# Two more token tiles turned by DMA instead of TensorE, one weight load moved back, and two gate tiles moved forward

## The chip, the cores and the metric

The kernel runs on one core of one Trainium2 chip. The metric is the device time of one execution in microseconds (us); of several runs the median is given. A profile is one profiled execution of the same program; it has a time of its own.

## The reference

`x` has 2048 tokens of 512 values; `xn` is its layer norm. The output is `x + A(xn) + B(xn)`.

- A is a sliding local attention: `q`, `k`, `v` are `xn @ wqkv`, 32 heads of 16 values; each token attends to itself and to 7 tokens before it at a distance of 2 each (mask, softmax, sum); then `@ wo`.
- B is a gated unit with a spatial matrix: `z = gelu(xn @ w_in)` has two halves of 688 values. The first half is `z1`; the second is layer-normed over its 688 values to `z2`. Then `g = w_sp @ z2 + b_sp` mixes the tokens (2048 x 2048), and B is `(z1 * g) @ w_out`.

```python
xn = _layernorm(x, axis=-1)
return x + _A_ref(xn, A_wqkv, A_wo) + _B_ref(xn, B_w_in, B_w_sp, B_b_sp, B_w_out)
```

## The kernel before

**Tiles and stages.** The tokens are 16 tiles of 128. Everything stays on the chip between the stages.

1. *Norm and turn.* `x` is loaded in nine DMAs (`x0` to `x12`, lines 162 to 166). For tile i, VectorE takes mean and variance (`b`, `ag`), GpSimd the reciprocal root (`gr`), and VectorE writes the normalised tile into one of eight buffers (`n`, line 180; tiles 8 to 15 take the buffers of tiles 0 to 7 again, line 194). Matmuls need the tile turned, channels on the partitions, in `xnT`. Tiles below `NPE` (8) are turned by TensorE: four 128x128 turns into a PSUM bank (`T`, line 213), and ScalarE copies them out (`Tc`, line 216). The other tiles are turned by one DMA each (`t`, line 196) from SP's queue.
2. *z and y.* For each tile eight matmuls with 344 columns (line 231) make z2's half (`z`), and eight more make z1's half (`y`); ScalarE applies gelu (`h`, line 249, and `yg`, line 313). They need the weights `wz0`, `wz1` (ScalarE's queue) and `wy` (SP's queue).
3. *q, k, v.* Eight passes each (`k0` to `k7` and so on, line 324), 64 matmuls to a pair of dimensions; each pass needs all sixteen tiles of `xnT` and its weights (`wk`, `wq`, `wv`, lines 241 to 243). The copies out of PSUM are `kc`, `qc`, `vc` (line 337). Since the attention reaches over tile borders, small DMAs copy the halos (`kh0` to `kh3`, `vh`, lines 342 and 343).
4. *Attention on VectorE.* Products of q and k (`m`, line 358), folds (`f`, partly adding DMAs from GpSimd, line 366), logits (`p`), maximum (`X`), softmax, and the weighted sum of v (`a`, lines 425 to 438).
5. *Spatial mixing.* `M0` to `M15`, 32 matmuls each (line 467), with `w_sp` loaded and turned by eight DMAs (`W0` to `W7`, line 451) into three buffers; ScalarE adds the bias (`G`), VectorE multiplies with z1 (`g`), and a DMA turns the product (`U`, lines 473 to 476).
6. *Output.* `gf`, `re` and `ao` (lines 511, 516 and 523) add both parts in PSUM, then x is added and the result stored.

**What sets the order.** It is written out by hand. Five lists (`pe`, `act`, `dve`, `pool`, `sp`, lines 565 to 612) name the steps of each engine in order; each step has a list of steps that it needs, and the program is issued so that each engine gets its list. A step waits only for what it needs, but whatever follows it in the same list waits too. DMAs of one queue are issued in the order of the list, and SP's list holds the x loads, most weight loads, the transposes `t` and `W`, the halos of the first two k chunks and of v, the turns `U` and the stores.

PSUM holds three buffers of two banks (`mm`) for z, y, q, k, v and M, and two buffers of one bank (`aux`) for the turns. A buffer goes round: the fourth user waits for the reader of the first (`psum`, line 201). So the order of z and y tiles in TensorE's list also says whose gelu each one waits for.

Around the change TensorE's list is `T5 z4 T6 z5 T7 B z6 z7 y0 y1 z8 ... z14 k0`; `B` is the turn of the spatial bias (line 459), which ScalarE copies (`Bc`, line 461). SP's list is `... wk wq wv t8 ... t15 W0 kh0 W1 kh1 vh W2 ...`. `gf0` and `gf1` name the last users of the PSUM buffers that they take over (`EVM`, line 527).

Of the kernel before, what the change touches and what calls it, by code (L numbers as in the profile page):

```python
# [16 lines left out]
NT = S // P  # L17
# [25 lines left out]
def kernel(  # L43
# [15 lines left out]
    G = nc.gpsimd  # L59
# [3 lines left out]
    x2 = A_x.rearrange("b s d -> (b s) d")  # L63
# [42 lines left out]
    z2 = z2_r[:].rearrange("p (i f) -> p i f", i=NT)  # L106
# [43 lines left out]
    def op_(name, after, f):  # L150
        assert name not in do, name
        do[name], needs[name] = f, list(after)

    def tok(i):
        return f"Tc{i}" if i < NPE else f"t{i}"

    NPE = 8
    ALLX = [tok(i) for i in range(NT)]
    ALLN = [f"n{i}" for i in range(NT)]

# [18 lines left out]
    def norm(eng, i):  # L179
        eng.tensor_scalar(xn[i % 8], xs[:, i, :], mv[:, i, 0:1], rstd[:, i:i + 1], ALU.subtract, ALU.mult)  # L180
# [5 lines left out]
    for i in range(NT):  # L186
# [6 lines left out]
        else:  # L193
            op_(f"n{i}", [f"gr{i}"] + ([tok(i - 8)] if i >= 8 else []), lambda i=i: norm(V, i))
        if i >= NPE:
            op_(f"t{i}", [f"n{i}"], lambda i=i: SP.dma_start_transpose(xnT[:, :, i * P:(i + 1) * P], xn[i % 8]))
# [311 lines left out]
    def gated_full(i, start, stop, c=slice(0, D)):  # L508
        th, t0 = i // 8, (i % 8) * P
        for m in range(MF):  # L510
            PE.matmul(po[i][:, c], uT[th][:, m, t0:t0 + P], wout[:, m, c], start=(start and m == 0), stop=(stop and m == MF - 1))  # L511

    def gated_rest(tiles, start, stop):
        for i in tiles:
            r, t0 = 64 * (i // 2 % 2), (i % 8) * P
            PE.matmul(po[i], uT[i // 8][r:r + FREST, MF, t0:t0 + P], wout[r:r + FREST, MF, :],  # L516
                      start=start, stop=stop, tile_position=(r, 0))
# [6 lines left out]
                          start=(start and d == 0), stop=(stop and d == DH - 1), tile_position=(32 * g, 0))  # L524

    U = [[f"U{j}" for j in range(8 * th, 8 * th + 8)] for th in range(2)]
    EVM = [f"G{j}" for j in range(NT)] + ["Bc", "Tc4"]
    for n in (0, 1):
        op_(f"gf{n}", LO + U[0] + EVM, lambda n=n: [gated_full(i, True, False) for i in groups[n]])
        op_(f"re{n}", [f"gf{n}"], lambda n=n: gated_rest(groups[n], False, False))  # L530
# [28 lines left out]
    for n, c in enumerate(halves):  # L559
# [2 lines left out]
        op_(f"Sl{n}", [f"Fl{n}"], lambda n=n, c=c: (SP, A)[n].dma_start(out2[i * P:(i + 1) * P, c], o_of(i)[:, c]))  # L562


    pe = """wu T0a T0 z0a z0A T1 z0B T2 z1 T3 z2 T4 z3 T5 z4 T6 z5 T7 B z6 z7 y0 y1 z8 z9 z10 z11 z12 z13 z14
        k0 k1 q0 q1 z15 k2 k3 q2 q3 k4 k5 q4 q5 k6 k7 q6 q7
        v0 v1 v2 v3 v4 v5 v6 v7 y2 y3 y4 y5 y6 y7 y8 y9 y10 y11 y12 y13 y14 y15
        M0 M1 M2 M3 M4 M5 M6 M7 M8 M9 M10 M11 M12 M13 M14 M15
# [1 line left out]
    for n in pe:  # L570
# [19 lines left out]
    op_("GL", [], lambda: A.preload_act_table(ACT.Gelu_apprx_tanh))  # L590
    op_("EL", ["yg15"], lambda: A.preload_act_table_set("natural_log_exp_and_others"))

    act = """wz0 wz1 GL Tc0a Tc0 Tc1 Tc2 h0 Tc3 h1 Tc4 h2 Tc5 h3 Tc6 h4 Tc7 Bc h5 h6 h7 yg0 yg1 h8 h9 sq8 h10 h11 sq9 h12 h13 h14 sq10
        kc0 sq11 kc1 qc0 sq12 qc1 h15 kc2 sq13 kc3 sq14 qc2 sq15 qc3 kc4 kc5 qc4 qc5 kc6 kc7 qc6 qc7
        vc0 zn8 vc1 zn9 vc2 zn10 vc3 zn11 vc4 zn12 vc5 zn13 vc6 zn14 vc7 zn15
        yg2 yg3 yg4 yg5 yg6 yg7 yg8 yg9 yg10 yg11 yg12 yg13 yg14 yg15 EL
# [3 lines left out]
    for i in range(6, NT):  # L600
# [5 lines left out]
    OUT = [i for n in range(3) for i in groups[n]] + tail[:3]  # L606
    dve += [f"F{i}" for i in OUT] + ["Fl0", "Fl1"]
    pool = ["b16"] + [f"gr{i}" for i in range(NT)] + "zr0 zr4 f01 zr8 kh2 f10 zr12 kh3 f11 f20 f21 f30 f31".split()
    sp = """x0 x1 x2 x3 x4 x5 x6 x8 wy x12 wk wq wv t8 t9 t10 t11 t12 t13 t14 t15 W0 kh0 W1 kh1 vh
        W2 W3 LO0 LO1 W4 U0 W5 LO2 LO3 U1 U2 W6 LO4 U3 U4 W7 U5 U6 U7 U8 U9 U10 R0 U11 U12 U13 R1 U14 U15""".split()  # L610
    sp += [f"S{i}" for i in OUT] + ["Sl0"]
    act.append("Sl1")
# [52 lines left out]
```

## Time and profile before

| | |
|---|---|
| three runs | 201.16, 201.68 and 201.68 us, median 201.68 |
| the profiled execution | 201.17 us |
| its span, first to last instruction | 199.4 us |
| TensorE busy | 97% of the span |
| VectorE busy | 89% |
| ScalarE busy | 45% |
| mean traffic of the DMA engines | 163 GB/s |

The difference between the profiled execution's time and its span lies outside the program's instructions. In the profile PE is TensorE's matmuls and PEld its weight loads, DVE is VectorE, ACT ScalarE, POOL GpSimd and SP SyncE; a small q behind an engine is its instruction queue, which issues the DMAs. A row of the timeline and of the chain gives the start and the length in us; `x8` behind it says how many instructions it holds. "DMA to landing" is the time from the issue of a DMA to its semaphore. A row of a stretch gives its length, then for each engine the busy time and the number of instructions, then the clock granted to TensorE, the DMA share and GB/s.

### The profile page before, as it was taken

How to read it: one execution, taken by the hardware profiler on the slowest of the kernel's cores; microseconds unless marked ns; L12 is line 12 of the kernel's file. 1: busy time of each engine (PE TensorE's matmuls, PEld its weight loads, DVE VectorE, ACT ScalarE, POOL GpSimd, SP SyncE). 2: the span in 40 equal slices, each digit the busy share in tenths (PEclk: the TensorE clock that was granted, in tenths of full speed). 3: DMA queues.
4: the chain of work that ended last, by engine and by line, in shares of the span. 5: the costliest groups of instructions: out<-in, count | busy, mean ns of one | idle time of the engine just before them, and what ended most of it. 6: DMA issues, size and time to landing. Idle time of an engine off the chain costs nothing.

```text
span 199.4 us, 4530 instructions
## 1 busy us (share of the span) xinstructions
PE 194.3 (97%) x1935; PEld 122.5 (61%) x1935; DVE 177.5 (89%) x204; ACT 89.7 (45%) x130; POOL 39.0 (20%) x67
## 2 busy tenths in 40 slices
PE   7899999999999999999999999999999999999993
PEld 2576666666777766666666666666666654443441
DVE  4999895899898999988999999999999999997234
ACT  2597797795559996672542311112221110043000
POOL 5677122002999330330000000000000000000000
PEclk9999999999999999999999999999999999999999
DMA  5999476840977999998099999999996679914233
GB/s 163 349 361 230 89 123 139 144 81 0 196 132 140 197 196 147 185 167 168 11 234 229 188 168 227 237 123 258 198 230 60 118 219 233 154 19 133 81 105 105
DMA packets 68964, 32.58 MB, mean 163 GB/s; under 512 B 56912, under 2 KB 67024, under 8 KB 68816
## 3 DMA queue, kind: packets, MB, share of 16 engines
q1 hardware_dynamic: 65568, 24.12, 59.5%
q0 software_dynamic: 2176, 7.40, 20.0%
q10 hardware_dynamic: 1200, 0.77, 1.4%
q8 instruction: 15, 0.25, 0.5%
q14 instruction: 5, 0.04, 0.1%
HBM read 10.03 MB, written 2.10 MB: 61 GB/s over the span
## 4 chain that ended last, share of the span: by engine, by line
PE 95%; DMA 3%; DVE 1%; ACTq 0%; DVEq 0%; issue 0%
PE mm L467 37%; PE mm L324 21%; PE mm L231 19%; PE mm L523 7%; PE mm L511 7%; DMA wts<-in_B_w_in_dram 3%; PE aux L511 2%; PE mm L516 1%; PE aux L213 1%; ACTq L239 0%; DVE z L561 0%; DVEq L660 0%; DVE wsp L129 0%; PE aux L523 0%; DVE qk L139 0%
## 5 line engine op out<-in xcount | busy, mean ns | idle before, releaser
L467 PE MATMUL mm<-z,wsp 128*128 128x344 bf16 x512 | 74.8, 309 | 0.0
L467 PEld LDWEIGHTS <-wsp 128*128 128x128 bf16 x512 | 50.1, 98 | 24.6
L324 PE MATMUL mm<-xnT,wts 128*32 128x512 bf16 x768 | 41.9, 380 | 0.0
L231 PE MATMUL mm<-wts,xnT 128*128 128x344 bf16 x256 | 39.0, 309 | 0.5 <-ACT xnT L216 0.5
L324 PEld LDWEIGHTS <-wts 128*32 128x32 bf16 x768 | 29.5, 140 | 12.0 <-issue 0.6
L425 DVE TENSOR_TENSOR prod<-vp,a_sb 128x4096 bf16<-128x4096 bf16 x16 | 36.1, 2285 | 0.0
L481 ACT ACTIVATE qk<-mm,b_col 128x688 bf16<-128x688 f32 x16 | 13.3, 830 | 45.3 <-PE mm L467 38.3
L231 PEld LDWEIGHTS <-xnT 128*128 128x128 bf16 x256 | 24.4, 98 | 13.0 <-issue 1.0
L358 DVE TENSOR_TENSOR prod<-qk 128x4096 bf16<-128x4096 bf16 x12 | 27.0, 2288 | 1.8 <-DMA qk<-qk 1.6
L429 DVE TENSOR_TENSOR prod<-prod,prod 128x8192 bf16<-128x8192 bf16 x6 | 26.5, 4420 | 0.0
L337 ACT CAST qk<-mm 128x1024 bf16<-128x1024 f32 x16 | 16.2, 1012 | 7.8 <-PE mm L324 7.8
L313 ACT ACTIVATE z<-mm 128x688 bf16<-128x688 f32 x16 | 11.8, 748 | 5.7 <-PE mm L231 5.3
L366 POOL DMA_DIRECT2D prod<-prod x10 | 8.7, 1022 | 28.3 <-DVE zvar L282 16.0
L523 PE MATMUL mm<-wts,xnT 32*128 32x512 bf16 x192 | 14.2, 374 | 0.0
L511 PEld LDWEIGHTS <-qk 128*128 128x128 bf16 x85 | 8.2, 98 | 9.4 <-issue 0.8
L511 PE MATMUL mm<-wts,qk 128*128 128x512 bf16 x60 | 13.6, 379 | 0.0
L249 ACT ACTIVATE z<-mm 128x688 bf16<-128x688 f32 x16 | 11.9, 745 | 1.9 <-PE mm L231 1.8
L170 DVE BATCH_NORM_STATS2 stats<-z 128x6 f32<-128x512 bf16 x16 | 10.8, 673 | 1.7 <-DMA z<-in_A_x_dram 1.7
L523 PEld LDWEIGHTS <-xnT 32*128 32x128 bf16 x256 | 6.3, 93 | 7.7 <-issue 0.8
L556 DVE TENSOR_TENSOR z<-mm,wsp 128x512 bf16<-128x512 f32 x6 | 3.8, 684 | 8.0 <-PE mm L523 4.8
L550 ACT CAST z<-mm 128x512 bf16<-128x512 f32 x6 | 3.2, 598 | 13.7 <-PE mm L523 12.3
L177 POOL TENSOR_TENSOR rstd<-rstd,mhalf 128x1 f32<-128x1 f32 x16 | 9.0, 561 | 1.3
(82 smaller groups left out, 169.6 us busy)
## 6 DMA issues: line engine op xcount, KB each, us to landing
prod<-prod POOLq DMA_DIRECT2D x10, 512.0 KB, 7.6
wts<-in_A_wo_dram SPq DMA_DIRECT2D x4, 512.0 KB, 6.3
wsp<-in_A_x_dram SPq DMA_DIRECT2D x2, 1024.0 KB, 6.5
out_dram<-z SPq DMA_DIRECT2D x15, 128.0 KB, 1.8
wts<-in_A_wqkv_dram SPq DMA_DIRECT2D x3, 512.0 KB, 8.6
z<-in_A_x_dram SPq DMA_DIRECT2D x2, 512.0 KB, 6.4
wsp<-z POOLq DMA_DIRECT2D x2, 512.0 KB, 6.5
wsp<-wts POOLq DMA_DIRECT2D x2, 512.0 KB, 8.9
```

The costliest lines, as they stand in the source:

```text
L231: PE.matmul(t[:, hh, 0:FHALF], xnT[:, kc, i * P:(i + 1) * P], w_z[part][:, kc, hh * FHALF:(hh + 1) * FHALF], start=(kc == 0), stop=(kc == ...
L249: A.activation(z2[:, i, :].rearrange("p (a b) -> p a b", a=2), t[:, :, 0:FHALF], ACT.Gelu_apprx_tanh, **total)
L313: op_(f"yg{i}", [f"y{i}"], lambda: A.activation(z1u[:, i, 0:FH].rearrange("p (a b) -> p a b", a=2), t[:, :, 0:FHALF], ACT.Gelu_apprx_tanh))
L324: PE.matmul(t[32 * g:32 * g + 32, dd, :], w, r, start=(kc == 0), stop=(kc == C - 1), tile_position=(0, 32 * g))
L337: op_(f"{a}c{p}", [f"{a}{p}"], lambda: A.copy(home(a, p), t[:].rearrange("p d (t s) -> p d t s", t=2)))
L358: V.tensor_tensor(pr, q, k, ALU.mult)
L425: return lambda: V.tensor_tensor(dst, vp[:, :, th, off:off + GS], a_sb[:, th, W - 1 - w].unsqueeze(1).broadcast_to([P, DH, GS]), ALU.mult)
L429: return lambda: V.tensor_tensor(dst, dst, x, ALU.add)
L467: PE.matmul(t[:, hh, 0:FHALF], w[:, k, (j % 2) * P:(j % 2 + 1) * P], z2[:, k, hh * FHALF:(hh + 1) * FHALF], start=(k == 0), stop=(k == NT ...
L481: lambda: A.activation(gs[j % 3].rearrange("p (a b) -> p a b", a=2), t[:, :, 0:FHALF], ACT.Identity, bias=b_col[:, j:j + 1]))
L511: PE.matmul(po[i][:, c], uT[th][:, m, t0:t0 + P], wout[:, m, c], start=(start and m == 0), stop=(stop and m == MF - 1))
L523: PE.matmul(po[groups[n][g]], op[32 * g:32 * g + 32, th, d, s * P:(s + 1) * P], wo_r[32 * g:32 * g + 32, d, :], start=(start and d == 0), ...
```

## The change

`NPE` goes from 8 to 6: the turns `T6` and `T7` and their copies `Tc6` and `Tc7` go, and two DMA transposes `t6` and `t7` come, ahead of `t8` in SP's list. `wv` moves in SP's list from behind `wq` to behind `kh1`. In TensorE's list `B` follows `T5`, and `y0` and `y1` stand ahead of `z6` and `z7`; ScalarE's list follows that order. The last user of one `aux` buffer, which `EVM` names, is now `Tc5`.

```diff
-    NPE = 8
+    NPE = 6
...
-    EVM = [f"G{j}" for j in range(NT)] + ["Bc", "Tc4"]
+    EVM = [f"G{j}" for j in range(NT)] + ["Bc", "Tc5"]
...
-    pe = """wu T0a T0 z0a z0A T1 z0B T2 z1 T3 z2 T4 z3 T5 z4 T6 z5 T7 B z6 z7 y0 y1 z8 z9 z10 z11 z12 z13 z14
+    pe = """wu T0a T0 z0a z0A T1 z0B T2 z1 T3 z2 T4 z3 T5 B z4 z5 y0 y1 z6 z7 z8 z9 z10 z11 z12 z13 z14
...
-    act = """wz0 wz1 GL Tc0a Tc0 Tc1 Tc2 h0 Tc3 h1 Tc4 h2 Tc5 h3 Tc6 h4 Tc7 Bc h5 h6 h7 yg0 yg1 h8 h9 sq8 h10 h11 sq9 h12 h13 h14 sq10
+    act = """wz0 wz1 GL Tc0a Tc0 Tc1 Tc2 h0 Tc3 h1 Tc4 h2 Tc5 Bc h3 h4 h5 yg0 yg1 h6 h7 h8 h9 sq8 h10 h11 sq9 h12 h13 h14 sq10
...
-    sp = """x0 x1 x2 x3 x4 x5 x6 x8 wy x12 wk wq wv t8 t9 t10 t11 t12 t13 t14 t15 W0 kh0 W1 kh1 vh
+    sp = """x0 x1 x2 x3 x4 x5 x6 x8 wy x12 wk wq t6 t7 t8 t9 t10 t11 t12 t13 t14 t15 W0 kh0 W1 kh1 wv vh
```

## The prediction

> **What bounds the kernel now.** I read the page's busy shares first, then its chain that ended last, then the same chain in order of time.
>
> ```profile
> PE 194.3 (97%) x1935; PEld 122.5 (61%) x1935; DVE 177.5 (89%) x204; ACT 89.7 (45%) x130; POOL 39.0 (20%) x67
> PE 95%; DMA 3%; DVE 1%; ACTq 0%; DVEq 0%; issue 0%
> ```
>
> ```profile
> 12.33 0.22 PE aux L213 x4
> 12.55 1.17 PE mm L231 x8
> 13.72 0.22 PE aux L213 x4
> 13.94 1.17 PE mm L231 x8
> 15.11 0.22 PE aux L213 x4
> 15.45 12.94 PE mm L231 x88
> 28.38 7.07 PE mm L324 x128
> 35.45 1.27 PE mm L231 x8
> 36.72 34.70 PE mm L324 x534
> 71.43 16.44 PE mm L231 x112
> 87.87 74.67 PE mm L467 x512
> ```
>
> TensorE is busy for 194.3 of 199.4 us, 95% of the chain is its own work, and in the eleven rows each piece begins where the one before ended (between 15.33 and 15.45 runs B). So whatever leaves TensorE here shortens the program by its own length, provided that nothing else comes late; and every wait put into TensorE lengthens it by the whole wait. The other engines matter only through the times at which they hand something to TensorE.
>
> The rows at 12.33, 13.72 and 15.11 are T5, T6 and T7, four turns each; between them stand z4 and z5 (eight matmuls, 1.17 us). The row at 15.45 is eleven token tiles (z6, z7, y0, y1, z8 to z14): 12.94 / 11 = 1.176 us each. k0 begins at 28.38.
>
> **The change, part by part.**
>
> *Removed from TensorE: T6 and T7.* Two rows of 0.22 us: 0.44 us. B (one small turn, the 0.12 us between 15.33 and 15.45) only moves ahead of z4. The two copies Tc6 and Tc7 leave ScalarE, which is not in the chain there.
>
> *The price of one turn.* Each of these eight instructions has a longer duration by itself:
>
> ```profile
> L213 PE MATMUL aux<-ident,z x32: 219/219/230, 5.2 to 15.1; 128*128 128x128 bf16 x32
> ```
>
> One lasts 219 ns, but four fill 0.22 us of the chain: they are pipelined, 55 ns apart. I take 8 x 55 = 0.44 us; the other end would be 8 x 219 = 1.75 us, which the chain's rows speak against. The Trainium skill ("TensorE: Matmul & The Clock Gate", Part 4, PE-mode transpose) gives about 275 ns for a 128x128 turn in one kernel's context; taken as a price it would make the saving an estimated 2.2 us. The trace disagrees with that as a price: 0.22 us for four.
>
> *The new times on TensorE.* T5 ends at 12.55. Then B to 12.67, z4 to 13.84, z5 to 15.01, y0 to 16.19, y1 to 17.36; z6 starts at 17.36, z7 at 18.54, z8 at 19.71, z14 at 26.77, k0 at 28.38 - 0.44 = 27.94. These are the times by which the transposes t6 to t15 must have landed.
>
> *Added to SP's queue: t6 and t7, ahead of t8.* Two normalised tiles on VectorE, and the queue as it is now:
>
> ```profile
> 12.48 0.40 DVE L180 TENSOR_SCALAR z<-z,mv,rstd 128x512 bf16<-128x512 bf16 x1
> ...
> 19.82 0.41 DVE L180 TENSOR_SCALAR z<-z,mv,rstd 128x512 bf16<-128x512 bf16 x1
> ```
>
> ```profile
> 5.31 0.37 SPq L244 DMA_DIRECT2D wts<-in_B_w_in_dram  x1
> 6.71 0.37 SPq L163 DMA_DIRECT2D z<-in_A_x_dram  x1
> 7.12 0.75 SPq L241 DMA_DIRECT2D wts<-in_A_wqkv_dram  x1
> 7.92 1.02 SPq L242 DMA_DIRECT2D wts<-in_A_wqkv_dram  x1
> 8.98 1.52 SPq L243 DMA_DIRECT2D wts<-in_A_wqkv_dram  x1
> 14.87 11.09 SPq L196 DMA_TRANSPOSE xnT<-z  x8
> 26.05 4.72 SPq L451 DMA_TRANSPOSE wsp<-in_B_w_sp_dram  x1
> ```
>
> The first row is n6, which ends at 12.88; the second n14. SP issues nothing between 10.50 and 14.87, where t8 goes; without wv it is free from 8.94. So t6 is issued when n6 is done, at 12.9. How far apart the issues follow, by t12 and t15:
>
> ```profile
> 20.80 1.22 SPq L196 DMA_TRANSPOSE xnT<-z  x1
> ```
>
> ```profile
> 24.73 1.22 SPq L196 DMA_TRANSPOSE xnT<-z  x1
> ```
>
> Three steps take 3.93 us, 1.31 each; the four steps before, from 14.87 to 20.80, took 5.93, which is 0.69 more than 4 x 1.31. At 1.31 a step, t7 goes at 14.2, t8 at 15.5, t14 at 23.4 and t15 at 12.9 + 9 x 1.31 = 24.7, as now: the two added transposes fill the time in which SP waited. With the same 0.69 of stretches t15 goes at 25.4.
>
> *When they land.* Three times from issue to landing: of the eight transposes, of wq, of wv.
>
> ```profile
> DMA to landing us min/median/max: 2.4/2.6/4.7
> ```
>
> ```profile
> DMA to landing us min/median/max: 8.6/8.6/8.6
> ```
>
> ```profile
> DMA to landing us min/median/max: 10.1/10.1/10.1
> ```
>
> The shortest way is 2.4 us. t8 had the longest, 4.7 us (19.6): it stood behind wv, which landed at 8.98 + 10.1 = 19.1, 0.5 us before it. In the new order t6 stands behind wq, which lands at 7.92 + 8.6 = 16.5. The trace shows no transpose just behind wq, so both ends: 12.9 + 2.4 = 15.3 if nothing held it, 12.9 + 4.7 = 17.6 with t8's way. I take wq's landing plus 0.5, 17.0, since a transpose behind a load is what t8 was. z6 needs it at 17.36: 0.3 us to spare at my value, a wait of 0.25 at the upper end. t7 half a us later (17.5) against 18.54; t8 at 15.5 + 2.6 = 18.1 (20.2 by its old 4.7, a wait of 0.5) against 19.71; t14 at 23.4 + 2.4 = 25.8 against 26.77; t15 at 27.1 against 27.94, at 27.8 with the stretch. n14, which now waits for t6 to leave its buffer (behind it on VectorE stand n15, waiting for t7, and zt0), ran at 19.82; W0 is issued at 26.0 as now.
>
> *wv moved behind kh1.*
>
> ```profile
> 42.09 0.65 SPq L343 DMA_DIRECT2D qk<-qk  x1
> ```
>
> ```profile
> DMA packets 0, 0.00 MB, mean 0 GB/s; under 512 B 0, under 2 KB 0, under 8 KB 0
> ```
>
> The first row is kh1's second half; wv follows it, at 42.8. The second row is the stretch from 44.9 to 48.6: no DMA packet at all. Even its old 10.1 us gives 53; v0 starts at 71.43 - 8 x 1.735 = 57.5 (34.70 / 20 = 1.735 us per pass), or 57.1 after the change. Behind it in SP's queue stands vh, which waits for the last v copy, long after. Nothing is paid; without the empty stretch there would still be 4 us.
>
> *y0 and y1 ahead of z6 and z7.* Same matmuls; what they need:
>
> ```profile
> wts<-in_B_w_in_dram SPq DMA_DIRECT2D x1, 688.0 KB, 6.7
> ```
>
> ```profile
> 13.07 0.75 ACT L249 ACTIVATE z<-mm 128x688 bf16<-128x688 f32 x1
> ```
>
> wy, issued at 5.31, landed at 12.0; y0 now starts at 15.01. y0's PSUM buffer waits for h3, the second row (13.07 to 13.82), which now follows Tc5 and Bc, a few tenths later, before 14.3. Cost nothing. h6 and h7 come about 2 us later; VectorE takes them up (zt6, zt7) only after zt0 to zt5 and four zn, all of which stand behind n15.
>
> *Behind k0.* The first handover is kh0, then VectorE's long list, then W2 (with its time to landing) and VectorE's last wait:
>
> ```profile
> 35.85 4.50 DVE L358 TENSOR_TENSOR prod<-qk 128x4096 bf16<-128x4096 bf16 x2 [1.65 <-DMA qk<-qk]
> ```
>
> ```profile
> 98.04 4.10 SPq L451 DMA_TRANSPOSE wsp<-in_B_w_sp_dram  x1
> ```
>
> ```profile
> DMA to landing us min/median/max: 6.2/6.2/6.2
> ```
>
> ```profile
> 188.15 2.48 DVE L556 TENSOR_TENSOR z<-mm,wsp 128x512 bf16<-128x512 f32 x4 [4.77 <-PE mm L523]
> ```
>
> VectorE's list starts on kh0, which follows kc1 on ScalarE, so it comes 0.44 earlier unless W0's packets hold it; at worst it stays. W2 is issued when VectorE has the last logits, at 98.04, and lands at 104.2; M4 starts at 87.87 + 4 x 4.667 = 106.5, so 2.3 us to spare, 1.9 if VectorE stays where it is. The last row shows VectorE waiting 4.77 us for TensorE's ao2 with its attention done; it keeps over 4 of them. So the saving reaches the end.
>
> **Sum.** -0.44 with 0 of waits: 201.17 of the profiled execution becomes 200.73. That execution equals the lowest of the three runs (201.16, 201.68, 201.68; mean 201.51); on the mean the forecast is 201.07, and I name 201.1. That is -0.22%; about 0.3% (0.6 us) is what a measurement of this kernel can tell from no change.
>
> **The rivals.**
>
> *A stall of the transposes under z6: slower.* The trace has one such stall:
>
> ```profile
> 17.40:18.90 1.50, 1.50 (x13) 0.99 (x11) 1.50 (x7) 0.84 (x2) 1.18 (x3) 1.00 1.64 36
> ```
>
> ```profile
> q8 instruction: 1, 0.02, 70.4%
> ```
>
> The last row is the stretch from 16.90 to 17.00: one packet of instructions that takes 0.704 x 16 x 0.1 = 1.13 us. Right behind it, from 17.40 on, the traffic falls to 36 GB/s for 1.5 us while t8 and t9 are under way. If it hits t6, t6 lands at 17.0 + 1.5 = 18.5, z6 waits 1.15, and the time is 0.44 less and 1.15 more: +0.7, 201.9 by the profile's time. It turns the change into a loss once t6 lands after 17.36 + 0.44 = 17.8. Against it: if the packet is fetched when TensorE has come equally far in its instructions, it comes later, since eight matmuls with eight loads are gone from in front of it: 1.18 - 0.44 = 0.74 us, at 17.7, when t6 and t7 have landed. The Trainium skill ("Runtime: NRT & Kernel Launch", Instruction fetch mechanics) calls the crossing of such a block mostly hidden. By that the fetch would add nothing to the forecast; TensorE indeed shows no gap in the trace, but the transposes beside it do.
>
> *The tail of the queue eats the saving: no change.* SP issues a transpose every 1.31 us, TensorE consumes one in 1.18. If the stretch of 0.69 comes twice, t15 goes at 26.1 and lands at 28.5, k0 waits up to 0.5, and the sum is 201.2 by the profile's time; the same if t7 or t8 is caught by the packet at 17.7 and comes 0.4 to 0.6 late, as t8's old way would make it. For it: t8's margin is thin if it needs its old way. Against it: wv no longer stands in the queue, and without it fewer packets are ahead.
>
> *A turn costs its whole duration.* 8 x 219 ns: 199.4 by the profile's time. Only the pitch of 0.22 us per four speaks against it, but plainly.
>
> **Chances.** Forecast 0.62; saving eaten 0.20; stall under z6 0.13; turns dearer 0.05. The forecast's -0.22% lies near enough to -0.3% that I count 0.15 of its 0.62 as faster by over 0.3%: faster 0.05 + 0.15 = 0.20, within it 0.47 + 0.20 = 0.67, slower 0.13. The range takes in the forecast by the profile's time (200.73, less 0.1), the unchanged median (201.68) and a stall of the size of the saving and a little more: 200.6 to 201.9. The dear turns and the worst of the stall lie outside.
>
> **What would show it.** Right: between T5 and z4 only B, no gap before the rows of z6, z8 and k0, k0 at about 27.9, t6 issued at 12.9 and landed by 17.3, t15 issued by 25.4, a span of 199.0. Wrong: TensorE idle before z6 or k0 with a transpose of xnT as the releaser, a traffic gap before 17 us with t6 in it, or a gap before M4 with W2 late.

## The result, and the profile after

The changed kernel takes 202.97 us (median of 6 runs, 202.63 to 203.32) against 201.56 us before (6 runs, 201.14 to 201.78). The ratio is 1.0064, with a 95% interval of 1.0036 to 1.0092: slower by 0.64%, about 1.3 us, where 0.22% less was forecast. Its profiled execution took 202.63 us, with a span of 200.7.

The page of the changed kernel: busy shares, then the chain that ended last by engine and by line.

```profile
PE 193.9 (97%) x1927; PEld 121.1 (60%) x1927; DVE 177.5 (88%) x204; ACT 88.7 (44%) x128; POOL 39.0 (19%) x67
...
PE 89%; DMA 5%; DVE 4%; SPq 0%; issue 0%; DVEq 0%
PE mm L467 37%; PE mm L324 21%; PE mm L231 14%; PE mm L523 7%; PE mm L511 7%; DMA xnT<-z 3%; PE aux L511 2%; DVE stats L170 2%; DMA z<-in_A_x_dram 2%; PE mm L516 1%; DVE z L180 1%; DVE mv L173 1%; SPq L163 0%; DVE z L561 0%; DVEq L660 0%
```

TensorE lost 0.4 us of work, as it should. New in the chain is "DMA xnT<-z" with 3%, a transpose, with VectorE's norms ahead of it: before 18.7 us the chain no longer runs through TensorE. TensorE's timeline shows the place (start, length, and in brackets the idle time and what ended it).

```profile
12.56 0.39 PE L213 MATMUL aux<-ident,z 128*128 128x128 bf16 x4
12.88 0.18 PE L459 MATMUL aux<-ident,b 16*128 16x16 bf16 x1
12.99 4.84 PE L231 MATMUL mm<-wts,xnT 128*128 128x344 bf16 x32
18.71 10.67 PE L231 MATMUL mm<-wts,xnT 128*128 128x344 bf16 x72 [0.88 <-DMA xnT<-z]
29.31 0.88 PE L324 MATMUL mm<-xnT,wts 128*32 128x512 bf16 x12
```

T5, B, then z4, z5, y0, y1 (32 matmuls) run through; z6 starts at 18.71. By the pace of 1.176 us a tile it was due at 12.99 + 4.70 = 17.69, so it lost 1.02 us (0.88 by the row, which begins at the modelled end of the last matmul). The next two rows are t6's issue with its nine followers, and the time from t6's issue to its landing.

```profile
13.11 13.50 SPq L196 DMA_TRANSPOSE xnT<-z  x10
```

```profile
DMA to landing us min/median/max: 5.6/5.6/5.6
```

t6 landed 5.55 us after 13.11, at 18.66; wq had landed at 16.8. What happened between is shown first by stretches (length, busy time and count of each engine, clock, DMA share, GB/s), then by the queue that carries packets of instructions, from 16.60 to 16.70:

```profile
15.50:17.06 1.56, 1.56 (x12) 1.05 (x11) 1.56 (x7) 1.11 (x2) 1.32 (x3) 1.00 1.73 237
17.06:18.50 1.44, 0.77 (x6) 0.29 (x3) 1.44 (x5) 1.02 (x2) 1.01 (x4) 1.00 1.28 11
18.50:19.60 1.10, 0.89 (x7) 0.61 (x8) 1.10 (x5) 0.11 (x1) 0.88 (x3) 1.00 1.15 233
```

```profile
q8 instruction: 1, 0.02, 67.9%
```

The packet takes 0.679 x 16 x 0.1 = 1.09 us, from 16.61 to 17.70. From 17.06 on the traffic falls from 237 to 11 GB/s for 1.44 us, though t6, t7 and t8 had been issued and had not landed: the same picture as before the change, where wv, t8 and t9 were under way, now with t6. The next two rows are the DMA packets that start from 17.21 to 17.67, and those from 17.70, the end of the packet of instructions, to 18.47:

```profile
DMA packets 0, 0.00 MB, mean 0 GB/s; under 512 B 0, under 2 KB 0, under 8 KB 0
```

```profile
DMA packets 28, 0.01 MB, mean 9 GB/s; under 512 B 28, under 2 KB 28, under 8 KB 28
```

For half a us nothing starts. Then packets of 256 B go one after another, 0.03 us apart, about 30 until the others go on. A tile has 128 KB, and a sixteenth of it, which would be the share of one of the 16 DMA engines, is 32 such packets. Meanwhile 26 packets that had started from 17.04 to 17.20 stay open, and all end between 18.49 and 18.53. So it looks as if one share of the tile is done alone behind the packet of instructions, and the rest waits for it.

The end of the program is the second difference. SP closes the program with a list of waits, one entry after another, which takes in the semaphores that DMAs raise when they land. The last sum and store, and SP's waits for stores in that list (total, times, longest), before:

```profile
196.04 0.76 DVE L561 TENSOR_TENSOR z<-aux,wsp 128x256 bf16<-128x256 f32 x2 [0.28 <-PE aux L511]
...
196.82 0.37 ACTq L562 DMA_DIRECT2D out_dram<-z  x1
```

```profile
SPq L660 <- DMA out_dram<-z: 1.1, 3, 0.5
```

And after:

```profile
197.02 0.76 DVE L561 TENSOR_TENSOR z<-aux,wsp 128x256 bf16<-128x256 f32 x2 [0.29 <-PE aux L511]
...
197.81 0.36 ACTq L562 DMA_DIRECT2D out_dram<-z  x1
```

```profile
SPq L660 <- DMA out_dram<-z: 1.5, 1, 1.5
```

From the start of the last sum's row to the end of the span it was 3.34 us (199.38 - 196.04) and is 3.70 (200.73 - 197.02, unrounded). ScalarE's store is issued 0.78 to 0.79 us behind the sum and lands 1.6 us later in both. What differs is the list: before, SP waited three times for stores, 1.1 us in all, and was nearly through the list when the last one landed; after, it waits once, 1.5 us, and then works through the rest of the list.

### The profile page after: what moved, and what is told of

The parts are those of the page before. It is cut to its first block, busy times and chain, and to the rows that moved or that the text cites. A ratio compares the mean times of both kernels' runs of the same rounds, so it can differ in the third digit from the quotient of the medians.

```text
span 200.7 us, 4516 instructions
## 1 busy us (share of the span) xinstructions
PE 193.9 (97%) x1927; PEld 121.1 (60%) x1927; DVE 177.5 (88%) x204; ACT 88.7 (44%) x128; POOL 39.0 (19%) x67
## 4 chain that ended last, share of the span: by engine, by line
PE 89%; DMA 5%; DVE 4%; SPq 0%; issue 0%; DVEq 0%
PE mm L467 37%; PE mm L324 21%; PE mm L231 14%; PE mm L523 7%; PE mm L511 7%; DMA xnT<-z 3%; PE aux L511 2%; DVE stats L170 2%; DMA z<-in_A_x_dram 2%; PE mm L516 1%; DVE z L180 1%; DVE mv L173 1%; SPq L163 0%; DVE z L561 0%; DVEq L660 0%
## 5 line engine op out<-in xcount | busy, mean ns | idle before, releaser
L324 PEld LDWEIGHTS <-wts 128*32 128x32 bf16 x768 | 28.4, 138 | 13.2 <-issue 0.6
```

Source lines behind the costliest of these rows:

```text
L324: PE.matmul(t[32 * g:32 * g + 32, dd, :], w, r, start=(kc == 0), stop=(kc == C - 1), tile_position=(0, 32 * g))
```

## The experiments

The theory that they test: TensorE's wait for t6 is the loss; t6 is late because the packet of instructions (below: the packet) comes while it is under way. Rivals: t6 is late by its place behind a load, whatever the packet does; or the loss sits elsewhere. The theory on the end came with the second profile of each kernel.

**e1: z6 due later.**

```diff
-... B z4 z5 y0 y1 z6 z7 z8 ... v7 y2 y3
+... B z4 z5 y0 y1 y2 z6 z7 z8 ... v7 y3
```

> The changed kernel with y2 as well ahead of z6 and z7, so that z6 is due 1.17 us later (about 18.9 instead of 17.8). Theory: the loss is TensorE's wait of 0.88 us for t6, which lands at 18.66; then no wait before z6 is left and the time falls by about 0.9, to 202.1, or to 201.1 if the later start of the first z tiles (0.39 us in the profile of the change) was chance. Rival: the loss sits elsewhere (the start, the end); then the wait goes but the time stays within 0.3 of 202.97.

201.36 us against 201.57; ratio 0.9978 (0.9953 to 1.0002). TensorE's timeline:

```profile
12.91 16.58 PE L231 MATMUL mm<-wts,xnT 128*128 128x344 bf16 x112
29.42 0.88 PE L324 MATMUL mm<-xnT,wts 128*32 128x512 bf16 x12
```

112 matmuls from z4 to z14 without a gap, though t6 landed at 18.77, as late as in the changed kernel. The profiled execution took 201.54 us against the changed kernel's 202.63: 1.09 less, of which 1.02 are the wait and 0.08 an earlier z4. The wait for t6 is the larger part of the loss. The medians lie 1.6 apart, which is more than the wait; what the rest is, these runs don't show.

**e2: the packet earlier.**

```diff
-    [PE.matmul(aux[1][:], warm[:, 0:P], warm, ...) for _ in range(9)]
+    [PE.matmul(aux[1][:, 0:D // 2], warm[:, 0:P], warm[:, 0:D // 2], ...) for _ in range(18)]
```

> The changed kernel with the nine warm-up matmuls of 512 columns written as eighteen of 256: same work, 18 more instructions ahead of all others. Theory (instruction packet): t6 is late because the DMA engine that carries the packet of instructions (16.61 to 17.70) does its share of t6 last; the packet comes 18 instructions, about 1.3 us, earlier, at 15.3, and t6 lands near 17.4 instead of 18.66; the wait at z6 shrinks from 0.88 to under 0.2. Rival (queue): t6 is late because it stands behind wq's load; it lands at 18.5 to 18.8 as before and the wait stays 0.8 to 0.9, wherever the packet is.

202.53 us, ratio 1.0041 (1.0019 to 1.0063). The packet came at 15.43, 1.2 us earlier, and z6 did not wait. But t6 landed at 18.21, not at 17.4: the packet now fell on wq, which landed at 17.73, 2.2 us behind wk instead of 1.5, and t6 came 0.5 us behind it. In this execution z6 was due late (18.31, since the start was 0.6 late), so the missing wait alone shows little. What it does show is that a packet that comes earlier is paid by the load ahead of t6. That the added instructions moved the packet is not shown: e4, with nine warm-up matmuls, had it at 15.49, and e11, with the changed kernel's order up to y1, at 15.93.

**e3: one load more ahead of t6.**

```diff
-... wk wq t6 t7 ... kh1 wv vh
+... wk wq wv t6 t7 ... kh1 vh
```

> The changed kernel with wv back behind wq, ahead of t6: one more load of 512 KB ahead of the transposes. Queue rival: t6 lands 1.5 us later (a load's share of the rings), near 20.2, z6 waits 2.4, time 204.4. Theory (packet alone): the packet at 16.6 ends at 17.7 and t6 lands about 1 to 1.5 us behind it, or behind wv at 19.1 plus 0.5 where that is later: 19.5, z6 waits 1.7, time 203.8. If neither matters, 202.97.

204.05 us, ratio 1.0095 (1.0056 to 1.0135). t6 landed at 20.26:

```profile
20.31 9.95 PE L231 MATMUL mm<-wts,xnT 128*128 128x344 bf16 x67 [2.34 <-DMA xnT<-z]
```

The landing and the wait are those of the queue rival (20.2 and 2.4); the time lies between the two forecasts (204.4 and 203.8). Yet wv landed at 18.40, and t6 came 1.86 us behind it, not 0.5; the packet lay from 18.23 to 19.32, and t6 landed 0.94 behind its end. Both parts count: the added load and the packet.

**e4: the two other parts alone.** Tiles 6 and 7 are turned by TensorE again; wv and the y tiles stay where the change put them.

```diff
-    NPE = 6
+    NPE = 8
...
-... T5 B z4 z5 y0 y1 z6 z7
+... T5 z4 T6 z5 T7 B y0 y1 z6 z7
```

> The kernel before with the two other parts alone: wv behind kh1, y0 and y1 ahead of z6 and z7, tiles 6 and 7 still turned by TensorE. Theory: both cost nothing, 201.3 to 201.8, no wait of TensorE between 8 and 28 us, and wv lands ten us ahead of v0. Rival (a moved weight load or the new order shifts the early stage): z1 starts at 8.6 instead of 8.2 as in the profile of the change, and the time is 0.4 up, 202.0.

201.47 us, ratio 0.9988 (0.9958 to 1.0017), no wait between z1 and k0, wv landing at 47.3. Moving wv and the y tiles costs nothing that these runs can tell. z1 did start at 8.7 here, in a kernel whose early part is that of before, so the later start goes with the execution, not with the change.

**e5: only wk ahead of t6.**

```diff
-... wk wq t6 t7 t8
+... wk t6 t7 wq t8
```

> The changed kernel with wq's load behind t6 and t7 in SP's queue, so that only wk stands ahead of t6. Theory: t6 was late by two things, wq ahead of it and the packet of instructions that catches it; behind wk alone (landing at 15.3) it lands 0.5 us later, at 15.8 to 16.3, before the packet at about 16.6, and the wait at z6 (due at 17.8) is gone; time as e1, 201.2 to 201.5, unless t8 and t9, now behind wq, come late for z8 (20.1). Rival (the packet alone decides): the packet still catches t6 or t7, t6 lands near 18.7 and the time stays at 202.9.

203.88 us, ratio 1.0099 (1.0066 to 1.0132): a miss. t6 landed at 16.62, 0.5 behind wk, as expected, and z6 did not wait. But the packet (17.25 to 18.65) caught t7 (19.56), and t8, now behind wq and issued at 17.2, landed at 22.25:

```profile
14.85 7.17 PE L231 MATMUL mm<-wts,xnT 128*128 128x344 bf16 x48
22.29 8.34 PE L231 MATMUL mm<-wts,xnT 128*128 128x344 bf16 x56 [0.27 <-DMA xnT<-z]
```

The lateness was handed on to z8. Much of the rest is a slow start in this execution (z4 at 14.85 instead of 12.99); whether it belongs to this kernel or to its few runs stays open.

**e6: the packet later.**

```diff
-... for _ in range(9)]
+... for _ in range(4)]
```

> The changed kernel with four warm-up matmuls instead of nine, 10 instructions fewer ahead of everything (the warm-up's result is not used). Theory: the packet comes when about 177 to 205 instructions have been started, so 0.7 us later, at 17.3; t6 is through by then and lands 0.5 us behind wq, at 17.3, z6 waits 0.0 to 0.2; the time is 201.4 to 201.7 if the shorter warm-up costs nothing at the start. Rival (t6's lateness is its place behind wq): 18.5 to 18.8 again and a wait of 0.8. The packet may vary by more than the 0.7 us; then t6's landing still follows the packet's end by 0.9 to 1.0 us where the packet is ahead of t6's end.

203.12 us, ratio 1.006 (1.0031 to 1.009). The packet came at 17.75, t6 landed at 17.14, 0.48 behind wq (16.66), and no z tile waited; t8 was the one that the packet caught (issued at 15.74, landed 4.4 later). A DMA raises its semaphore in 16 steps; of t8's, fifteen came by 18.18 and the last at 20.12, so here one share alone was late. That is the theory's picture of t6, but z6 was due late here, at 19.09. The time did not fall, because the short warm-up cost more at the start:

```profile
6.23 1.33 PE L231 MATMUL mm<-wts,xnT 128*128 128x344 bf16 x4 [0.46 <-ACT xnT L216]
...
9.35 1.99 PE L231 MATMUL mm<-wts,xnT 128*128 128x344 bf16 x8
...
14.39 5.86 PE L231 MATMUL mm<-wts,xnT 128*128 128x344 bf16 x39
```

z0's first four matmuls take 1.33 us there, and z4 starts 1.4 us later than in the changed kernel. The packet came 1.14 later than there, so its moment may have followed the late start and not the missing instructions.

**e7 and e8: both kernels once more, unchanged.**

> The kernel before, once more, for its profile. If the start in the first profile (z1 at 8.2) was chance, z1 starts at 8.5 to 8.8 here and the span is 199.7 to 199.9. If the packet's time belongs to the program it comes at 16.8 to 17.3 again; if it varies from execution to execution, anywhere from 15.4 to 17.5.

> The changed kernel once more, for its profile. Theory: z6 waits for t6 again, by 0.7 to 1.1 us, and t6 lands 0.9 to 1.0 us behind the packet's end. Rival (the wait was chance of one execution): no wait at z6 and a time near 201.5.

The kernel before took 202.59 us this time, with z1 at 9.4 and the packet at 17.08; its end was 3.34 again. The changed kernel took 202.25:

```profile
12.66 4.84 PE L231 MATMUL mm<-wts,xnT 128*128 128x344 bf16 x32
18.45 10.67 PE L231 MATMUL mm<-wts,xnT 128*128 128x344 bf16 x72 [0.95 <-DMA xnT<-z]
```

The wait is there again (due at 12.66 + 4.70 = 17.36, started at 18.45), with the packet from 16.34 to 17.44 and t6 landing 0.97 behind it, at 18.41. This execution started as early as the first profile of before (T5 at 12.23 against 12.17), so the two can be subtracted: +1.09 for the wait, -0.44 for T6 and T7, +0.37 for the end (3.71), +0.06 for the start is 1.08; measured, 202.25 - 201.17 = 1.08.

All executions with tiles 6 and 7 turned by DMA, in one table (us; the load is the one just ahead of the first transpose; e10 to e12 are told below):

| run | packet | load lands | first transpose lands | z6 waits (by its row) |
|---|---|---|---|---|
| after | 16.61 to 17.70 | wq 16.80 | t6 18.66 | 0.88 |
| e8 | 16.34 to 17.44 | wq 16.55 | t6 18.41 | 0.95 |
| e1 | 16.71 to 17.80 | wq 16.91 | t6 18.77 | none (due later) |
| e3 | 18.23 to 19.32 | wv 18.40 | t6 20.26 | 2.34 |
| e2 | 15.43 to 16.67 | wq 17.73 | t6 18.21 | none (due 18.31) |
| e5 | 17.25 to 18.65 | wk 16.11 | t6 16.62 | none |
| e6 | 17.75 to 19.04 | wq 16.66 | t6 17.14 | none (due 19.09) |
| e10 | 17.20 to 18.19 | wq 17.29 | t6 19.15 | 0.95 |
| e11 | 15.93 to 17.43 | wq 16.61 | t6 18.46 | none (due later) |
| e12 | 16.90 to 17.99 | wq 16.66 | t5 17.14 | none (due later) |

Where the packet starts ahead of the load's end and ends behind it, the first transpose lands 0.94 to 1.03 us behind the packet's end (after, e8, e1, e3, e10, e11). In the other four rows it lands 0.5 us behind the load: in e2 the packet had ended before the load, and in e5, e6 and e12 it started behind it. There it caught a later transpose: t7 in e5, t8 in e6, t6 in e12 (landed at 19.00, 1.01 behind the packet's end, while z6 was due later). The single file of 30 to 32 packets of 256 B behind the packet's end stands in the traces of after, e1, e3, e8, e10, e11 and e12 alike.

**e9: the end alone.** Two tiny DMAs are added to the kernel before, into a spare tile that nobody reads.

```diff
+    for n in range(2):
+        op_(f"N{n}", [], lambda n=n: SP.dma_start(spare[:, n, :], x2[0:P, n * 8:(n + 1) * 8]))
...
-... kh1 vh
+... kh1 N0 N1 vh
```

> The kernel before with two tiny DMAs (x's columns into a spare tile that nobody reads) behind kh1, where SP waits for 30 us: as many DMAs on SP and ACT as the changed kernel has, 89 instead of 87. Theory (the end): the eight DMA semaphores go round, so two more DMAs put ScalarE's last store on the semaphore that the closing list of waits asks first instead of nearly last, and the rest of the list follows after the landing; from the last DVE row to the end of the span 3.70 instead of 3.34, time +0.36: 201.9 to 202.0 where before is 201.6. Rival (the longer end belongs to the transposes or is chance): 3.34 and no change.

201.73 us against 201.43; ratio 1.0012 (0.9987 to 1.0036), which the interval doesn't tell from no change. The profile does: the last sum at 196.01, as before, and the span 199.7 instead of 199.4; the end is 3.70, and the wait list is that of the changed kernel.

```profile
SPq L665 <- DMA out_dram<-z: 1.4, 1, 1.4
```

In the trace the DMAs of SP and ScalarE take eight semaphores in turn. The last store raises semaphore 101 here and in the changed kernel, and 108 before; SP's list begins with 101 after two others and ends with 109, one entry every 0.06 us where it needn't wait.

**e10: the end undone.** The changed kernel with `wv N0 ... N5 vh`.

> The changed kernel with six such DMAs behind wv: 95 DMAs, so that the last store is on the same semaphore as in the kernel before. Theory: z6 still waits 0.9 to 1.1 for t6, but the end is 3.34 again; 0.36 less than the changed kernel, 202.5. Rival: 202.97 and an end of 3.7.

202.24 us against 201.43; ratio 1.0035 (1.0014 to 1.0056). The end is 3.33 again, on semaphore 108, and the wait for t6 is still there:

```profile
19.20 10.67 PE L233 MATMUL mm<-wts,xnT 128*128 128x344 bf16 x72 [0.95 <-DMA xnT<-z]
```

z6 was due at 13.41 + 4.70 = 18.11, so it waited 1.09. The ratio says +0.70 us (0.28 to 1.13); -0.44 and 1.09 make 0.65.

**e11: both causes removed.** e1 with seven such DMAs, `wv N0 ... N6 vh`.

> Both causes removed: y2 ahead of z6 and z7 as in e1, and seven tiny DMAs, 96 in all, so that the last store is on the last semaphore of the list. Theory: no wait for t6, end 3.28 to 3.34, so what is left is the forecast's own term: 0.44 less than before and up to 0.06 from the end, 201.05 to 201.15 where before is 201.57, and at least 0.3 less than e1. Rival (the end costs nothing): as e1, 201.36.

200.96 us against 201.43; ratio 0.9966 (0.9938 to 0.9993): 0.47 us below the kernel before by the medians, 0.14 to 1.25 by the interval. No wait, the store on semaphore 109, 3.25 us from the last sum to the end:

```profile
12.80 16.51 PE L233 MATMUL mm<-wts,xnT 128*128 128x344 bf16 x112
...
195.78 0.76 DVE L566 TENSOR_TENSOR z<-aux,wsp 128x256 bf16<-128x256 f32 x2 [0.28 <-PE aux L516]
```

**e12: one tile further.** `NPE = 5`, `... z3 B z4 y0 y1 y2 y3 z5 z6 z7 ...`, six such DMAs.

> Theory taken one tile further: tiles 5 to 15 turned by DMA, y0 to y3 ahead of z5, z6 and z7, six tiny DMAs (96 in all). T5 leaves TensorE too, 0.22 more. z5 is due at 18.5 and t5 lands at 18.2 to 18.7 if the packet catches it as it caught t6; t15 lands at about 28.4 against 29.2 for k0's fourth matmul. Time 200.85 where before is 201.57. Rival (the tail of the queue): t13 to t15 come late, z13, z14 or k0 wait 0.2 to 0.6, 201.1 to 201.5.

201.03 us, ratio 0.9981 (0.9952 to 1.001), unclear. Its profile is the shortest of all (span 198.9, no wait, M0 0.2 earlier than in e11, which is T5's share); 6 of its 12 runs lie at 201.3 to 202.5 and 6 at 200.4 to 200.8. No transpose came late, so the rival isn't shown either; the spread may be that of the start, below.

## Why the prediction was wrong

- **The saving of 0.44 us was right.** e11, with both costs gone, is 0.47 us below before by the medians (0.14 to 1.25), where 0.44 and 0.06 to 0.09 from the end were to be had. The profiles are sharper: from T5's start to M0's, by the timeline, it is 75.53 us before (12.17 to 87.70) and 75.07 in e11 (12.37 to 87.44), 0.46 less. So a turn costs its pitch, 55 ns, and the rival with 219 ns, which would have saved 1.75, falls.
- **"t6 lands at 17.0", half a us behind wq, was right without the packet** (e6: 0.48; e5: 0.51 behind wk). By these figures the margin of 0.3 us, thin as it was, would have held; no run shows it, since z6 was due later where t6 came early.
- **The step that failed is the one against the first rival:** "it comes later, ... at 17.7, when t6 and t7 have landed". So the sum went with "0 of waits", and the wait was 1.02 and 1.09. The packet came at 16.61 and 16.34. It is not fetched when TensorE has come equally far: 203 and 185 matmuls and weight loads had started when it came in the two profiles of the kernel before, 183 and 185 in those of the changed kernel, and 167 to 203 over all fourteen profiles, a spread of over 2 us of this program. With the spread taken into account the packet's time could not exclude t6, and the stall under z6 deserved far more than 0.13; a single profile of before could not show it. The price given for it (a wait of 1.15) was near what was measured.
- **The trace before was read too kindly.** I took t8's 0.5 us behind wv as the way of a transpose behind a load, and saw the stall only under t8 and t9. But wv itself was caught: it landed 2.51 us behind wq there (19.05 and 16.54), against 1.46 in e3, where the packet caught t6 instead. What is under way when the packet comes is late, load or transpose: wv by 1.05 us here, wq by 0.7 in e2, t6 by 1.4. The change put t6 where wv had stood.
- **A term was missing: the end, 0.37 us.** I counted what the two new transposes do to the queue and to the buffers, but not that two DMAs more turn the round of eight semaphores, and with it the order in which the closing list meets the last store. That gives back 0.84 of the gain, in a place where the diff changes nothing.
- **The queue behind t6 was right:** t15 was issued at 25.4 and landed at 27.8, ahead of k0; wv landed at 47.8; z8 to k0 did not wait; VectorE's handovers behind k0 held.
- **What stays open:** wait and end, less the saving, make 1.0 us; the medians differ by 1.4, with 0.7 to 1.9 in the interval. The rest may be the start, which varies between executions of one kernel. What sets the packet's moment within its 2 us is not settled either; e2 and e6, one profile each, don't show that the number of instructions does. That one DMA engine does its share of t6 only behind the packet, while the others wait, is borne out by the single file of about 30 packets, a sixteenth of a tile, and by the packets that stay open meanwhile. The trace does not name the engines, so it is not fully shown, and why the others wait is open: of t6's sixteen steps in the changed kernel one came at 17.29 and fifteen from 18.57 to 18.66, but of t8's in e6 fifteen came in time.

## What to carry to other kernels

A transpose that TensorE needs within a few tenths of a us of its landing must be given room for one packet of instructions, here 1.4 us (1.86 less 0.5 behind the load), or work that is ready must stand ahead of it, as y2 in e1. And when DMAs are added, look at the end too: which semaphore the last store raises, and how much of the closing list comes behind it.

## What the runs showed of the hardware that I had not expected

- **Packets of instructions and transposes.** The Trainium skill ("Runtime: NRT & Kernel Launch", Instruction fetch mechanics) calls the crossing of an instruction block mostly hidden. The trace agrees for TensorE's own stream, which shows no gap from it, and not for the transposes beside it: 1.09 us of packet, 1.44 us of almost no traffic, and a landing of t6 1.86 us behind the load instead of 0.5.
- **The start has two forms.** The same four matmuls of z0 in the kernel before, in its first profile and in e7:

```profile
6.21 0.76 PE L231 MATMUL mm<-wts,xnT 128*128 128x344 bf16 x4 [0.46 <-ACT xnT L216]
```

```profile
6.34 1.30 PE L231 MATMUL mm<-wts,xnT 128*128 128x344 bf16 x4 [0.61 <-DMA wts<-in_B_w_in_dram]
```

The slow form lasts until about 10 us and puts z2 1.4 us later (11.05 against 9.61), while the granted clock of the profile reads 1.00 in both. It would make most of the spread of the runs of before (200.96 to 203.48 beside e9 to e12), but only two of its executions were profiled, one of each form, so that is not shown. The Trainium skill ("TensorE: Matmul & The Clock Gate", Part 1) says that the array runs at half rate until it has been busy through a window of about 3.4 us. The trace agrees with a nearly doubled time per matmul (the next row starts 1.10 us behind these four in e7, 0.59 before), and e6, with less than half of the warm-up, had the slow form in its profile; which executions get it with the full warm-up no run here shows.
